# Moving steps of the second and third chunk in a fused attention and MLP kernel

## The chip, the cores and the metric

The kernel runs on one core of a Trainium2 chip. A core has a tensor engine (PE in the profile; PEld is its loading of weights), a vector engine (DVE), a scalar engine (ACT), a general engine that also issues transfers (POOL) and a sync engine that issues transfers (SP). Each takes its instructions in the order in which the program lists them and waits at an instruction until what it needs is there. Matrix products write to PSUM, eight banks that are numbered 0 to 7 here; the other data lie in SBUF. The metric is the device time of one execution in microseconds (us).

## What is computed

A linear attention with decay over 4 batches, 8 heads, 768 positions and head size 64, and behind it an MLP with a "snake" activation over the 3072 tokens. The reference, cut to its core:

```python
for b in range(nb):                     # 12 blocks of 64 positions
    sl = slice(b * block, (b + 1) * block)
    qb, kb, vb = (q[:, :, sl].copy(), k[:, :, sl].copy(), v[:, :, sl].copy())
    intra = np.einsum('bhic,bhjc->bhij', qb, kb) * Dmask[None]
    intra = np.einsum('bhij,bhjd->bhid', intra, vb)
    inter = np.einsum('bhid,bhde->bhie', qb * lam_pow[None], kv_state)
    out[:, :, sl] = intra + inter
    kb_dec = kb * rev_pow[None]
    kv_state = lam_block[None, :, None, None] * kv_state + np.einsum('bhsd,bhse->bhde', kb_dec, vb)
...
h = x @ w_in                            # 512 -> 2048
s = np.sin(alpha * h)
g = h + s * s / (alpha + 1e-09)
return (g @ w_out).astype(np.float32)   # 2048 -> 512
```

## The kernel before

**Tiling.** The 768 positions are cut into six chunks t = 0 to 5 of 128. A chunk of all four batches gives a group g = t of 512 tokens for the MLP. While PE does the MLP of group g, the attention of chunk g + 1 is spread between its products, so that its output `xt[g + 1]` is there when group g + 1 begins. A chunk has two halves of 64 positions (`blk`), and its batches come in two pairs (`pr`).

**The MLP.** For each of 16 slices f of the inner size, `hidden(g, f)` issues four products of 128x512 into one bank (L453), then on ACT the sine (L456) and, where `squarer` names ACT, the square (L461). `finish(g, f)` issues the square on DVE where `squarer` names DVE (L469), and always DVE's `gall` (L470), which reads the bank and so frees it. The second product is cut into units: `project(g, m, part)` is four products (L481) over `gall` f = 4 part to 4 part + 3 for the tokens of batch m. Units wait in the list `behind`; `run(n)` issues the next n. The unit with part 3 copies the sum out of PSUM (L488 on DVE or L490 on ACT) and queues the store. In group 0, `squarer` gives DVE the squares of f = 3, 5, 7, 9 and 11. The units of group 0 come in an order written out at L596; the last nine are (3,1), (0,2), (1,2), (2,2), (3,2), (3,3), (2,3), (0,3), (1,3).

**The attention of a chunk t.** 
- q and k are turned to have the head size in the partitions: on PE with a copy behind (`turn`, L275, copies L277 and L279; `turns_pair`, L289, copies L292), or by a transfer on SP's queue (`turn_by_dma`, L252).
- `decay_k` (POOL, L236) makes `kdec`; `states` (L369) multiplies it with v into four banks.
- `update(t, blk, pr)` adds this to the decayed state on DVE (L345; for chunk 1's second half four smaller instructions, L349), then POOL decays the new state for the next use (`decay_state`, L334) and casts it (`cast_state`, L338).
- `scores` (L389) multiplies k with q into F banks; `masks` (DVE, L396) reads them.
- `outputs_first` (L403) multiplies the states with q into O banks, all but one product; `outputs` adds that product and the masked scores with v (L428); `leave` (DVE, L435) writes `xt`.

Scores, states, turns and outputs of a chunk share banks. For chunk 1 the banks are passed by hand: its second pair's states use banks 4 and 2, its scores 5 and 0, its O banks 4 and 2 again. For later chunks they are `AB`, banks 4 to 7: states, the turned q, scores and O take them one after the other, and each must have been read before the next is written.

**The order around the change.** Group 0's loop over f (L598 to L626) also holds chunk 1's first pair of batches. Behind it stands a straight stretch for chunk 1's second pair (L627 to L659), where the calls `run(n)` place projection units of group 0 between the steps. Then the loop over g begins. In it, for group 1, `feed(g)` gives steps that are issued ahead of `hidden(g, i)`, `slots(g)` those behind it, then `run` issues as many units as i occurs in `units`, then `finish`. `own` names where units of group 1 itself are added to the list. `hidden(1, 11)` has chunk 2's `outputs_first` in its middle, behind its products and its sine.

**Loads.** `load` and `load_w_out` issue transfers on POOL's queue, which also does the decays and casts in program order. `load(t, nm, 2, 4)` of k and q are two transfers each (L101, L102).

Of the kernel before, what the change touches and what calls it, by code (L numbers as in the profile page):

```python
# [15 lines left out]
def kernel(  # L16
# [16 lines left out]
    NT = S // T  # L33
# [3 lines left out]
    NFC = DFF // P  # L37
# [53 lines left out]
    def load_w_out(i):  # L91
        nc.gpsimd.dma_start(out=w_out_sb[i][:],
                            in_=moe_w_out[i * 512:(i + 1) * 512, :].rearrange("(f p) d -> p f d", p=P))

    def load(t, nm, b0, b1):
        dst, src = NAT[nm]
        to = dst[t][:, b0:b1, :, :].rearrange("p b h e -> p (b h) e")
        by_head = src[b0:b1, :, t * T:(t + 1) * T, :].rearrange("b h p e -> p (b h) e")
        n = H * (b1 - b0)
        if t and nm != "v" and b0 == 2:  # L100
            nc.gpsimd.dma_start(out=to[:, 0:n - 1, :], in_=by_head[:, 1:n, :])  # L101
            nc.gpsimd.dma_start(out=to[:, n - 1:n, :], in_=by_head[:, 0:1, :])  # L102
        else:
            nc.gpsimd.dma_start(out=to, in_=by_head)  # L104
# [99 lines left out]
    V, G, A = nc.vector, nc.gpsimd, nc.scalar  # L204
# [17 lines left out]
    def home(t, blk):  # L222
        return SB[2 if blk else t % 2]
# [106 lines left out]
    def pair(tile, pr):  # L330
        return tile[:, 2 * pr:2 * pr + 2]

    def decay_state(n, pr):
        nc.gpsimd.tensor_tensor(out=pair(SD, pr), in0=pair(S_of[n], pr), op=ALU.mult,  # L334
                                in1=L64[:, pr].unsqueeze(1).unsqueeze(3).broadcast_to([P, 2, HP, D]))

    def cast_state(n, pr, dst):
        nc.gpsimd.tensor_copy(out=pair(dst, pr), in_=pair(S_of[n], pr))  # L338
# [94 lines left out]
    def leave(t, pr, blks=(0, 1)):  # L433
        for blk in blks:
            nc.vector.tensor_tensor(out=xview(t)[:, 2 * pr:2 * pr + 2, blk, :, :], in0=att["O", t, pr, blk],  # L435
                                    in1=Eb, op=ALU.mult)
# [4 lines left out]

    def squarer(g, f):
        if g == 0:
            return V if f in (3, 5, 7, 9, 11) else A
        return A

    H0 = (0, 1, 2, 3, 5, 6, 7, 4, 0, 1, 3, 5, 0, 1, 5, 0)
# [1 line left out]
    def hidden(g, f, between=None):  # L449
        hps = bank("hps", H0[f] if g == 0 else (0, 5, 4, 2)[f] if g == 1 and f < 4 else AB[0] if g == 1 and f == 15 else AB[f + 1] if g == 2 and f < 2 else HB[(f + 2) % 3] if g == 1 else HB[(16 * g + f + 1) % 3])  # L450
        w = w_in_sb[f // 4]
        for c in range(NDC):
            nc.tensor.matmul(out=hps[:], lhsT=w[:, c, (f % 4) * P:(f % 4 + 1) * P],  # L453
                             rhs=xt[g][:, c, :], start=(c == 0), stop=(c == NDC - 1))
        s_sb = mlps.tile([P, GRP], BF16, name="s_sb")
        nc.scalar.activation(out=s_sb[:], in_=hps[:], func=ACTF.Sin, scale=alpha_sb[:, f:f + 1])  # L456
        if between:
            between()
        s2 = mlps.tile([P, GRP], BF16, name="s2")
        if squarer(g, f) is A:  # L460
            nc.scalar.activation(out=s2[:], in_=s_sb[:], func=ACTF.Square)  # L461
        elif squarer(g, f) is G:
            nc.gpsimd.tensor_tensor(out=s2[:], in0=s_sb[:], in1=s_sb[:], op=ALU.mult)
        hps_of[g, f] = (hps, s_sb, s2)
# [19 lines left out]

    def store(g, m):
        o_sb = outp.tile([P, DM], FP32, name="o_sb")
        if g < NT - 2 and (g or m < 2):
            nc.vector.tensor_copy(out=o_sb[:], in_=ops_of.pop((g, m))[:])  # L488
        else:
            nc.scalar.copy(out=o_sb[:], in_=ops_of.pop((g, m))[:])  # L490
        held.append((m * S + g * T, o_sb))
        if g:
            put_held()

    def put_held():
        while held:
            row, o_sb = held.pop(0)
            nc.sync.dma_start(out=out[row:row + T, :], in_=o_sb[:])
# [93 lines left out]
    def run(n):  # L592
        for _ in range(min(n, len(behind))):
            behind.pop(0)()
# [3 lines left out]
    for f in range(NFC):  # L598
        hidden(0, f)
        if f in (1, 10):  # L600
            states1(0, f // 10, 2 if f == 10 else 4)
        if f == 10:
            decay_k(1, 0, 2)
            decay_state(1, 0)
            cast_state(1, 0, home(1, 0))
            load_w_out(2)
            load(1, "q", 2, 4)
            load_w_out(3)
            load(2, "v", 0, 2)
        if f in (11, 12):  # L610
            run(1)
        if f == 12:
            turns_pair(1, "k", 0, 4, (A, A))
        if f == 13:
            turn(1, "q", 0, 2, A)
            turn(1, "q", 1, 3, V)
        if f == 14:
            scores(1, (0,), (4, 2))
            masks(1, 0)
        if f == 15:  # L620
            run(1)
            states(1, (0,), (3, 4))
            finish(0, 14)
            update(1, 0, 0)
        if f != 14:
            finish(0, f)  # L626
# [11 lines left out]
    leave(1, 0)  # L638
    states(1, (1,), (4, 2))
    update(1, 0, 1)  # L640
    run(3)
    turn(1, "q", 2, 5, A)
    turn(1, "q", 3, 0, V)
    load(2, "k", 0, 2)
# [2 lines left out]
    scores(1, (1,), (5, 0))  # L647
    masks(1, 1)
    load(2, "k", 2, 4)
    run(1)  # L650
    outputs_first(1, (1,), (4, 2))
    load(2, "q", 0, 2)
    load(2, "q", 2, 4)
    run(1)
    outputs(1, (1,))
    leave(1, 1)
    run(1)
    decay_state(1, 0)
    pair_ready(2, 0)  # L659


    def slots(g):
        t = g + 1
        d = {i: [] for i in range(NFC)}
        if g == 1:
            at = dict(KV=6, F=9, O=12)
        else:
            at = dict(KV=4, F=8, O=12)
        d[at["KV"]] += [(states, t)]
        for n in range(4):  # L670
            d[at["KV"] + ((0, 0, 1, 2)[n] if g == 1 else n)] += [(update, t, n // 2, n % 2)]
        d[at["F"]] += [(scores, t), (masks, t, 0)]
        d[at["F"] + 1] += [(masks, t, 1)]
        d[at["O"]] += [(outputs, t), (leave, t, 0)]
        d[at["O"] + (g > 1)] += [(leave, t, 1)]
        return d

    def feed(g):
        t = g + 1
        d = {i: [] for i in range(NFC)}  # L680
        if g == 1:
            d[2] += [(turn_by_dma, 2, 0, "k"), (pair_ready, 2, 1), (decay_state, 1, 1), (turn_by_dma, 2, 1, "k"), (turn_by_dma, 2, 0, "q")]
            d[7] += [(put_held,)]
            d[8] += [(turns_pair, 2, "q", 2, AB[0], (A, A))]
        if t + 1 < NT:
            if g == 1:
                d[7] += [(new_chunk, 3)] + [(load, 3, nm, b, b + 2) for nm, b in (("v", 0), ("k", 0), ("v", 2))]
                d[8] += [(load, 3, nm, b, b + 2) for nm, b in (("k", 2), ("q", 0), ("q", 2))]
            else:
                a = 6 if g == 2 else 2  # L690
                d[a] += [(new_chunk, t + 1)] + [(load, t + 1, nm, b, b + 2) for nm, b in (("v", 0), ("k", 0), ("v", 2))]
                d[a + 2] += [(load, t + 1, nm, b, b + 2) for nm, b in (("k", 2), ("q", 0), ("q", 2))]
            d[12] += [(turn_by_dma, t + 1, 0, "k"), (turn_by_dma, t + 1, 1, "k")]
            d[13] += [(pair_ready, t + 1, 0)]
            d[14] += [(turn_by_dma, t + 1, 0, "q"), (turn_by_dma, t + 1, 1, "q")]
            d[15] += [(pair_ready, t + 1, 1)]
        return d

    for g in range(1, NT + 1):
        if g < NT:  # L700
            gall[g] = gbp.tile([P, NFC, GRP], BF16, name="gall")
        at = slots(g) if g + 1 < NT else {}
        fd = feed(g) if g + 1 < NT else {}
        if g + 1 < NT:
            new_xt(g + 1)
        own = {5: (0, 0), 8: (0, 1), 13: (0, 2)} if g == 1 else {}
        units = [1, 3, 5, 8, 13] if g == 1 else [i for i in range(NFC) if g > 2 or i not in (0, 1, 3)]
        for i in range(NFC):
            if g == NT and not behind:
                break  # L710
            if i in own:
                queue_units(g, [own[i]])
            for a in fd.get(i, []):
                a[0](*a[1:])
            if g > 1 and g + 1 < NT and i == 12:
                outputs_first(g + 1)
            if g < NT:
                hidden(g, i, (lambda: outputs_first(2)) if (g, i) == (1, 11) else None)
            for a in at.get(i, []):
                a[0](*a[1:])  # L720
            run(units.count(i))
            if g < NT:
                finish(g, i)
        if g < NT:
            queue_units(g, [(m, part) for m in range(B - 1 if g == NT - 1 else B) for part in range(4)][len(own):])
# [31 lines left out]
```

## Time and profile before

| what | value |
|---|---|
| times of three runs | 211.74, 211.49, 210.94 us; median 211.49 |
| the profiled execution's own time | 210.82 us |
| its span, first to last instruction | 209.0 us |
| granted PE clock | 0.997 of full speed |
| chain that ended last, share by engine | PE 80%, DVE 11%, ACT 4%, DMA 2% |
| gall on DVE (L470) | 96 instructions, 745 ns each |
| sine (L456) and square (L461) on ACT | 684 and 629 ns each |

The profile is of one execution. Its views used here: the page (busy time by engine), the instructions in order of time with like neighbours merged, busy time by stretch, and the chain of waits that ended last. Starts are in us from the span's start. The modelled end of a product lies behind the start of the next one, as products are pipelined, so the prediction works with starts.

### The profile page before, as it was taken

The numbers are of one execution on the slowest core, as the hardware profiler recorded it, in microseconds if no ns is written. First come the engines' busy times: TensorE is split into PE (matmuls) and PEld (weight loads), VectorE is DVE, ScalarE is ACT, GpSimd is POOL, SyncE is SP. The second block draws the span as 40 slices with busy tenths as digits, with TensorE's granted clock in tenths as the row PEclk, the third lists the DMA queues.
The fourth block names the chain that finished last, engine by engine and source line by source line (L and its number), as shares of the span: only waits on it lengthen the run. The fifth ranks groups of instructions, "written<-read, shape, count | busy, mean of one in ns | idle before, by whom it ended". The sixth has DMA issues, their size and how long they took to land.

```text
span 209.0 us, 5363 instructions
## 1 busy us (share of the span) xinstructions
PE 201.0 (96%) x2243; PEld 98.7 (47%) x2243; DVE 132.9 (64%) x218; ACT 143.1 (68%) x239; POOL 107.0 (51%) x111
## 2 busy tenths in 40 slices
PE   7999998999998999999999999999999999999993
PEld 2664444544453544445444444445444444444452
DVE  6794999473778868968547968556868544444000
ACT  4788989213999699765776775776675787887121
POOL 8989939979939993999986850002000000000000
PEclk9999999999999999999999999999999999999998
DMA  7999999999997999699999998701101101110212
GB/s 140 156 170 207 207 159 178 185 179 135 127 311 50 145 127 161 99 175 161 106 150 145 209 103 130 174 0 53 50 3 53 50 0 50 55 50 0 100 59 93
DMA packets 98794, 24.60 MB, mean 118 GB/s; under 512 B 90946, under 2 KB 95826, under 8 KB 98770
## 3 DMA queue, kind: packets, MB, share of 16 engines
q0 software_dynamic: 76176, 13.24, 86.7%
q1 hardware_dynamic: 20512, 10.50, 24.4%
q10 hardware_dynamic: 2082, 0.52, 1.4%
q8 instruction: 17, 0.28, 0.5%
q14 instruction: 7, 0.06, 0.1%
HBM read 27.27 MB, written 6.29 MB: 161 GB/s over the span
## 4 chain that ended last, share of the span: by engine, by line
PE 80%; DVE 11%; ACT 4%; DMA 2%; issue 1%; ACTq 0%
PE ops L481 37%; PE hps L453 33%; DVE gall L470 4%; DMA raw_k<-in_k_dram 2%; PE O_ps L403 2%; ACT s_sb L456 2%; ACT s L461 2%; PE hps L505 2%; DVE s L469 2%; DVE STm L304 2%; PE KV_ps L369 2%; PE O_ps L428 1%; PE F_ps L389 1%; DVE STm L396 1%; DVE xt L316 1%
## 5 line engine op out<-in xcount | busy, mean ns | idle before, releaser
L470 DVE SCALAR_TENSOR_TENSOR gall<-s,r_sb,hps 128x512 bf16<-128x512 bf16 x96 | 71.2, 745 | 45.0 <-ACT s L461 44.8
L453 PE MATMUL hps<-xt,w_in 128*128 128x512 bf16 x384 | 95.7, 379 | 1.2 <-DVE gall L470 0.5
L481 PE MATMUL ops<-w_out,gall 128*128 128x512 bf16 x368 | 92.4, 380 | 0.4 <-DVE gall L470 0.4
L456 ACT ACTIVATE s_sb<-hps,alpha_sb 128x512 bf16<-128x512 f32 x96 | 65.2, 684 | 32.1 <-PE hps L453 31.9
L461 ACT ACTIVATE s<-s_sb 128x512 bf16<-128x512 bf16 x91 | 57.3, 629 | 2.9
L453 PEld LDWEIGHTS <-w_in 128*128 128x128 bf16 x384 | 36.6, 98 | 44.1 <-issue 1.9
L481 PEld LDWEIGHTS <-gall 128*128 128x128 bf16 x368 | 34.6, 98 | 41.2 <-DVE gall L470 0.9
L236 POOL TENSOR_TENSOR kdec<-kn,R 128x1024 bf16<-128x1024 bf16 x12 | 22.8, 1924 | 3.2 <-DMA kn<-in_k_dram 3.2
L338 POOL CAST sb<-S 128x512 bf16<-128x512 f32 x20 | 12.3, 618 | 21.8 <-DVE S L345 20.6
L334 POOL TENSOR_TENSOR SD<-S,L 128x512 f32<-128x512 f32 x16 | 17.1, 1066 | 10.6 <-DVE S L345 10.5
L435 DVE TENSOR_TENSOR xt<-O_ps,Etab 128x512 bf16<-128x512 f32 x20 | 12.8, 685 | 6.3 <-PE O_ps L428 6.3
L104 POOL DMA_DIRECT2D vn<-in_v_dram x13 | 14.8, 1153 | 0.5 <-DMA w_in<-in_moe_w_in_dram 0.5
L396 DVE TENSOR_TENSOR STm<-F_ps,C 128x512 bf16<-128x512 f32 x20 | 12.8, 685 | 0.1
L488 DVE COPY o_sb<-ops 128x512 f32<-128x512 f32 x14 | 9.6, 689 | 4.2 <-PE ops L481 4.2
L490 ACT COPY o_sb<-ops 128x512 f32<-128x512 f32 x9 | 5.2, 577 | 9.7 <-PE ops L481 9.7
L345 DVE TENSOR_TENSOR S<-SD,KV_ps 128x512 f32<-128x512 f32 x16 | 10.8, 683 | 0.4 <-PE KV_ps L369 0.3
L128 PE MATMUL hps<-fill 128*128 128x256 bf16 (+1 forms) x40 | 9.7, 352 | 1.5 <-DVE fill L121 1.5
L277 ACT COPY QKT<-T_ps 128x512 bf16<-128x512 bf16 x9 | 5.2, 584 | 6.4 <-PE T_ps L275 6.4
L104 POOL DMA_DIRECT2D qn<-in_q_dram x8 | 8.8, 1099 | 0.3 <-issue 0.3
L104 POOL DMA_DIRECT2D kn<-in_k_dram x7 | 7.7, 1093 | 0.1
L403 PEld LDWEIGHTS <-sb 64*64 64x64 bf16 x320 | 4.3, 108 | 6.3 <-issue 6.3
L403 PE MATMUL O_ps<-QKT,sb 64*64 64x64 bf16 x320 | 5.9, 195 | 1.0 <-DVE STm L396 1.0
(75 smaller groups left out, 114.5 us busy)
## 6 DMA issues: line engine op xcount, KB each, us to landing
out_dram<-o_sb SPq DMA_DIRECT2D x23, 256.0 KB, 2.2
vn<-in_v_dram POOLq DMA_DIRECT2D x11, 256.0 KB, 7.5
w_out<-in_moe_w_out_dram POOLq DMA_DIRECT2D x4, 512.0 KB, 11.3
w_in<-in_moe_w_in_dram POOLq DMA_DIRECT2D x3, 512.0 KB, 11.6
kn<-in_k_dram POOLq DMA_DIRECT2D x5, 256.0 KB, 7.0
qn<-in_q_dram POOLq DMA_DIRECT2D x5, 256.0 KB, 9.9
kn<-in_k_dram POOLq DMA_DIRECT2D x5, 240.0 KB, 6.4
qn<-in_q_dram POOLq DMA_DIRECT2D x5, 240.0 KB, 9.0
```

What stands on the lines that cost most here:

```text
L104: nc.gpsimd.dma_start(out=to, in_=by_head)
L236: nc.gpsimd.tensor_tensor(out=kdec[t][:, b0:b1, :, :], in0=kn[t][:, b0:b1, :, :], in1=R[:, o:o + H].unsqueeze(1).unsqueeze(3).broadcast_to ...
L334: nc.gpsimd.tensor_tensor(out=pair(SD, pr), in0=pair(S_of[n], pr), op=ALU.mult, in1=L64[:, pr].unsqueeze(1).unsqueeze(3).broadcast_to([P, ...
L338: nc.gpsimd.tensor_copy(out=pair(dst, pr), in_=pair(S_of[n], pr))
L396: nc.vector.tensor_tensor(out=st[:, hd], in0=att["F", t, pr, hd], op=ALU.mult, in1=of_mask(C64, t, pr, hd).unsqueeze(1).broadcast_to([P, 2 ...
L403: nc.tensor.matmul(out=att["O", t, pr, blk][halves(h % 2), u, h // 2, :], lhsT=home(t, blk)[halves(half), 2 * pr + m // HP, m % HP, :], rh ...
L435: nc.vector.tensor_tensor(out=xview(t)[:, 2 * pr:2 * pr + 2, blk, :, :], in0=att["O", t, pr, blk], in1=Eb, op=ALU.mult)
L453: nc.tensor.matmul(out=hps[:], lhsT=w[:, c, (f % 4) * P:(f % 4 + 1) * P], rhs=xt[g][:, c, :], start=(c == 0), stop=(c == NDC - 1))
L456: nc.scalar.activation(out=s_sb[:], in_=hps[:], func=ACTF.Sin, scale=alpha_sb[:, f:f + 1])
L461: nc.scalar.activation(out=s2[:], in_=s_sb[:], func=ACTF.Square)
L470: nc.vector.scalar_tensor_tensor(out=gall[g][:, f, :], in0=s2[:], scalar=r_sb[:, f:f + 1], in1=hps[:], op0=ALU.mult, op1=ALU.add)
L481: nc.tensor.matmul(out=ops[:], lhsT=gall[g][:, f, m * P:(m + 1) * P], rhs=w_out_sb[part][:, f % 4, :], start=(f == 0), stop=(f == NFC - 1))
```

## The change

The diff moves work between engines and along the queues; no operation is added or left out.

```diff
     def squarer(g, f):
         if g == 0:
-            return V if f in (3, 5, 7, 9, 11) else A
+            return V if f in (1, 3, 5, 7, 9) else A
         return A
...
-        if g < NT - 2 and (g or m < 2):
+        if g < NT - 2 and (g or m < 3):
             nc.vector.tensor_copy(out=o_sb[:], in_=ops_of.pop((g, m))[:])
...
             cast_state(1, 0, home(1, 0))
+            load(1, "q", 2, 4)
             load_w_out(2)
-            load(1, "q", 2, 4)
             load_w_out(3)
...
     update(1, 0, 1)
-    run(3)
+    run(1)
     turn(1, "q", 2, 5, A)
     turn(1, "q", 3, 0, V)
     load(2, "k", 0, 2)
     run(1)
     update(1, 1, 1)
     scores(1, (1,), (5, 0))
     masks(1, 1)
     load(2, "k", 2, 4)
-    run(1)
     outputs_first(1, (1,), (4, 2))
     load(2, "q", 0, 2)
     load(2, "q", 2, 4)
-    run(1)
+    run(2)
     outputs(1, (1,))
     leave(1, 1)
-    run(1)
-    decay_state(1, 0)
+    run(2)
     pair_ready(2, 0)
...
         if g == 1:
-            at = dict(KV=6, F=9, O=12)
+            at = dict(KV=5, F=9, O=12)
...
-        d[at["F"]] += [(scores, t), (masks, t, 0)]
-        d[at["F"] + 1] += [(masks, t, 1)]
+        if g > 1:
+            d[at["F"]] += [(scores, t), (masks, t, 0)]
+        d[at["F"] + (g > 1)] += [(masks, t, 1)]
...
-            d[2] += [(turn_by_dma, 2, 0, "k"), (pair_ready, 2, 1), (decay_state, 1, 1), (turn_by_dma, 2, 1, "k"), (turn_by_dma, 2, 0, "q")]
+            d[2] += [(turn_by_dma, 2, 0, "k"), (pair_ready, 2, 1), (decay_state, 1, 0), (decay_state, 1, 1), (turn_by_dma, 2, 1, "k"), (turn_by_dma, 2, 0, "q")]
             d[7] += [(put_held,)]
             d[8] += [(turns_pair, 2, "q", 2, AB[0], (A, A))]
+            d[9] += [(scores, 2), (masks, 2, 0)]
         if t + 1 < NT:
             if g == 1:
-                d[7] += [(new_chunk, 3)] + [(load, 3, nm, b, b + 2) for nm, b in (("v", 0), ("k", 0), ("v", 2))]
-                d[8] += [(load, 3, nm, b, b + 2) for nm, b in (("k", 2), ("q", 0), ("q", 2))]
+                d[6] += [(new_chunk, 3)] + [(load, 3, nm, b, b + 2) for nm, b in (("v", 0), ("k", 0), ("v", 2))]
+                d[7] += [(load, 3, nm, b, b + 2) for nm, b in (("k", 2), ("q", 0), ("q", 2))]
...
-        own = {5: (0, 0), 8: (0, 1), 13: (0, 2)} if g == 1 else {}
-        units = [1, 3, 5, 8, 13] if g == 1 else [i for i in range(NFC) if g > 2 or i not in (0, 1, 3)]
+        own = {8: (0, 0), 10: (0, 1), 13: (0, 2)} if g == 1 else {}
+        units = [1, 3, 4, 8, 10, 13] if g == 1 else [i for i in range(NFC) if g > 2 or i not in (0, 1, 3)]
```

Put in the order of PE's work: in the straight stretch one unit instead of three stands ahead of q's turn, scores and `outputs_first` follow each other directly, and two units stand behind each of `outputs_first` and `outputs`; six units of group 0 run there instead of seven. In group 1 the three left run behind f = 1, 3 and 4, the group's own first units behind f = 8, 10 and 13 instead of 5, 8 and 13. Chunk 2's states come behind f = 5 instead of f = 6, its scores ahead of f = 9 instead of behind it. On DVE both pairs of masks of chunk 2 then lie between the `gall` of f = 8 and that of f = 9, and the copy of unit (2,3) comes to it from ACT. On POOL the load of q's second pair goes ahead of that of the third slice of w_out, a decay of the state goes behind the two `kdec` of chunk 2, and chunk 3's loads go one step of the loop ahead. SP's order is the same.

## The prediction

> **What bounds the kernel now.** I read the engine table of the page first, then a table of busy time by stretch, then the instructions in order of time where the tensor engine (PE) pauses (start and length in us, engine, line, and in brackets the idle time before and what ended it). A group of four PE products of 128x512, 0.865 us, is called a block below: (2.76 - 0.38)/11 = 0.216 us each, from the row of twelve at 41.81 further down and the 0.39 of a single one at 63.39.
>
> ```profile
> span 209.0 us, 5363 instructions
> PE 201.0 (96%) x2243; PEld 98.7 (47%) x2243; DVE 132.9 (64%) x218; ACT 143.1 (68%) x239; POOL 107.0 (51%) x111
> 69.10:80.00 10.90, 10.90 (x178) 5.28 (x170) 8.04 (x14) 9.61 (x17) 10.02 (x10) 1.00 2.43 139
> ```
>
> PE is busy 96% of the span, and from 69.1 us on it has no gap (10.90 of 10.90; columns are length, then PE, PEld, DVE, ACT, POOL). The amount of PE work doesn't change. So the change is worth the PE pauses it removes ahead of 69.1 less those it makes, and I walk PE through its new order. The profiled run took 210.82 us, 1.82 more than its span and 0.67 less than the median of 211.49; I make the sum against the span and carry the difference over.
>
> **The squares of group 0.** f = 1 moves from ACT to DVE, f = 11 from DVE to ACT.
>
> ```profile
> 29.64 0.69 ACT L456 ACTIVATE s_sb<-hps,alpha_sb 128x512 bf16<-128x512 f32 x1 [0.60 <-PE hps L453]
> 29.72 2.13 DVE L469 TENSOR_TENSOR s<-s_sb 128x512 bf16<-128x512 bf16 x1
> 32.69 1.02 PE L453 MATMUL hps<-xt,w_in 128*128 128x512 bf16 x4 [0.47 <-DVE gall L470]
> 33.18 0.57 ACT L277 COPY QKT<-T_ps 128x512 bf16<-128x512 bf16 x1
> 33.79 0.39 PE L389 MATMUL F_ps<-QKT 64*64 64x64 bf16 x25
> ```
> ```profile
> 29.60:33.80 4.20, 3.65 (x30) 2.02 (x29) 4.16 (x6) 4.09 (x8) 4.13 (x4) 1.00 1.84 187
> ```
>
> The square of f = 11 took 2.13 us on DVE, and f = 14's products then waited 0.47 for a bank (0.63 in starts, since a modelled end lies 0.16 behind the next start). That wait goes. But the next 64x64 work, the scores at 33.79, starts 0.04 after ACT's copy of q (33.18 + 0.57 = 33.75), and ACT was busy 4.09 of the 4.20 us before it. That copy doesn't come sooner: its row of ACT work starts at 29.64 with f = 12's sine, which waits for PE. PE comes to the scores 0.63 sooner and waits there 0.63 longer. I cost this part at nothing. The added square fits into the 0.60 of ACT idle ahead of 29.64, and ACT is relieved of f = 1's before. On DVE, the square of f = 1 lies ahead of an in-order row that PE doesn't wait for.
>
> **Second chunk: 41.8 to 50.6.** One unit (a block) of the projection moves out of this stretch into the loop behind it; scores and O-first become adjacent, and two units follow each.
>
> ```profile
> 41.81 2.76 PE L481 MATMUL ops<-w_out,gall 128*128 128x512 bf16 x12
> 42.84 0.68 DVE L345 TENSOR_TENSOR S<-SD,KV_ps 128x512 f32<-128x512 f32 x1
> 44.41 0.61 PE L275 MATMUL T_ps<-iden,qn 128*128 128x128 bf16 x8
> 44.85 1.03 PE L481 MATMUL ops<-w_out,gall 128*128 128x512 bf16 x4
> 45.06 0.42 DVE L279 COPY QKT<-T_ps 128x512 bf16<-128x512 bf16 x1 [1.54 <-PE T_ps L275]
> 45.40 1.11 DVE L349 SCALAR_TENSOR_TENSOR S<-S,L,KV_ps 128x128 f32<-128x128 f32 x4
> 45.81 0.45 PE L389 MATMUL F_ps<-QKT 64*64 64x64 bf16 x32
> 46.19 1.04 PE L481 MATMUL ops<-w_out,gall 128*128 128x512 bf16 x4
> 48.75 0.46 PE L428 MATMUL O_ps<-STm,vn 64*64 64x64 bf16 x32
> 49.14 1.04 PE L481 MATMUL ops<-w_out,gall 128*128 128x512 bf16 x4
> ...
> 50.61 1.89 PE L453 MATMUL hps<-xt,w_in 128*128 128x512 bf16 x8 [0.43 <-DVE xt L435]
> ```
> ```profile
> 47.23 0.62 PE O_ps L403 x31
> ```
>
> New walk: block (3,1) 41.81 to 42.68; the turn of q, 0.44 (44.41 to 44.85), to 43.12; block (0,2) to 43.98; a change to 64x64 costs 0.10 (45.81 less 44.85 + 0.865), so scores at 44.08, and their 32 products take some 0.27 of the 0.38 to 46.19, the rest being the way back to 128 rows. O-first would start at 44.35. Its second product writes the bank that L349 reads. DVE is in order: L345 until 43.52, the copy L279 until some 43.86, L349 (overlapping 0.08) until 44.90. So PE goes on at 44.95, a **new wait of 0.60** that before was covered by a block: L349 ended at 46.51, O-first came after 47. O-first from there 0.61 (the chain's 0.62 for the visit): 45.56; two units to 47.29, with 0.10 to 47.39; outputs, 0.39 (48.75 to 49.14), to 47.78; two units to 49.51. xt came 1.86 after the outputs' start (50.61 less 48.75), so at 49.25: covered by 0.26, and the wait at 50.61 (0.61 in starts, 49.14 + 0.865 = 50.00) is gone. Before, with one unit more: 50.61 - 0.865 = 49.74. **Gain 0.23**: 0.61 and one change of shape (about 0.2) less 0.60.
>
> **The two loads that change places.** q must be there at 42.68, w_out(2) at 43.12.
>
> ```profile
> L92 POOL DMA_DIRECT2D w_out<-in_moe_w_out_dram x1: 823/823/823, 33.3 to 33.3; - x1
> DMA to landing us min/median/max: 8.0/8.0/8.0
> ```
> ```profile
> L101 POOL DMA_DIRECT2D qn<-in_q_dram x1: 1204/1204/1204, 34.1 to 34.1; - x1
> DMA to landing us min/median/max: 9.0/9.0/9.0
> ```
> ```profile
> DMA to landing us min/median/max: 8.0/9.6/13.0
> ```
>
> w_out(2) landed at 41.3, q at 43.1. Swapped, q is issued at 33.3 and w_out(2) behind q's two issues at about 35.1 (estimate: 1.2 and half of it). If the queue keeps its order and its rate, the second of the two lands where the second did, 43.1: just in time, and a delay up to 0.60 goes into the wait for L349. I take zero. The ends: w_out(2) after 8.0 us again, nothing; after the 13.0 of the slowest of the three loads behind 20 us, 48.05, a wait of 4.9. This is the largest unknown. The row says that landings kept the order of issue; the Trainium skill, "DMA: Bandwidth & Descriptors", section "Two DMAs through the same engine are not ordered", says that nothing orders transfers across the 16 DMA engines. By that rule w_out(2) could share its time with w_out(3) behind it, which is the rival on the slower side below; by the row the sum stays.
>
> **Second group: 50.6 to 69.1.**
>
> ```profile
> 59.34 0.73 PE L369 MATMUL KV_ps<-vn,kdec 64*64 64x64 bf16 x64
> 60.01 1.04 PE L453 MATMUL hps<-xt,w_in 128*128 128x512 bf16 x4
> 61.08 0.69 ACT L456 ACTIVATE s_sb<-hps,alpha_sb 128x512 bf16<-128x512 f32 x1 [0.29 <-PE hps L453]
> 62.34 1.05 ACT L292 COPY QKT<-T_ps 128x512 bf16<-128x512 bf16 x2
> 63.39 0.39 PE L481 MATMUL ops<-w_out,gall 128*128 128x512 bf16 x1 [0.39 <-DVE gall L470]
> 64.67 0.75 DVE L470 SCALAR_TENSOR_TENSOR gall<-s,r_sb,hps 128x512 bf16<-128x512 bf16 x1 [0.46 <-ACT s L461]
> 65.33 1.28 DVE L396 TENSOR_TENSOR STm<-F_ps,C 128x512 bf16<-128x512 f32 x2
> 67.07 0.21 PE L403 MATMUL O_ps<-QKT,sb 64*64 64x64 bf16 x1
> 68.53 0.66 PE L403 MATMUL O_ps<-QKT,sb 64*64 64x64 bf16 x59 [0.38 <-DVE STm L396]
> 69.12 1.04 PE L453 MATMUL hps<-xt,w_in 128*128 128x512 bf16 x4
> ```
>
> Two waits go: 0.55 at 63.39 (0.39 and 0.16), where unit (0,1) ran before f = 7's gall; and 1.43 between 67.07 and 68.53, where O-first waited for the masks to free its banks. New walk from f0 at 49.51: six f and three units, 9 x 0.865, to 57.29; states at 57.39, 0.67 (59.34 to 60.01), so f6 at 58.06, f7 58.93, turn 59.79, f8 60.23, unit (0,0) 61.10 to 61.96, scores possible at 62.06. They write the bank that the two copies L292 read. ACT: f6's sine 1.07 after f6's start (61.08 less 60.01), 59.13; f7's sine 1.26 later (61.08 to 62.34 is a sine and a square), 60.39; the copies end 2.31 behind that sine, as before (63.39 less 61.08): 62.70. Scores at 62.75, a **new wait of 0.69**. Then f9 63.42, f10 64.28, unit (0,1) 65.15, f11 66.01, O-first possible at 66.98. DVE: f8's gall 1.28 behind the copies (64.67 less 63.39), 63.98; four masks from 64.64, 1.28 a pair, to 67.13. O-first's last bank is free at 67.18, **0.20 of wait** left; its last group takes 0.59 (68.53 to 69.12), to 67.77; f12 needs f9's gall, which DVE now has behind the masks, 67.05 + 0.75 = 67.80: f12 at 67.85. Against 69.12 that is **1.27 sooner**. By terms: 0.23 + 0.55 + 1.43 - 0.69 - 0.20 - 0.08 = 1.24; I take 1.25. The copy of unit (2,3) from PSUM moves from ACT to DVE, under the wait of DVE for ACT's squares.
>
> **What hides the rest.** The state decay that POOL has moved, and chunk 3's loads one step sooner:
>
> ```profile
> 52.82 3.79 POOL L236 TENSOR_TENSOR kdec<-kn,R 128x1024 bf16<-128x1024 bf16 x2
> 60.90 1.04 POOL L334 TENSOR_TENSOR SD<-S,L 128x512 f32<-128x512 f32 x1 [3.29 <-DVE S L345]
> 75.34 3.79 POOL L236 TENSOR_TENSOR kdec<-kn,R 128x1024 bf16<-128x1024 bf16 x2
> 79.53 0.66 PE L369 MATMUL KV_ps<-vn,kdec 64*64 64x64 bf16 x58
> ```
>
> Even if POOL were no sooner, kdec ends a decay sooner than at 56.61, at 55.6, and the two decays at 57.7, ahead of DVE's first need of them at about 57.9. Uncovered they would cost up to 1.04. Behind that POOL waited 3.29 for DVE at 60.90; this need now comes some 2 us sooner, so the six loads, and kdec at 75.34, follow sooner. They must: kdec of chunk 3 ended at 79.13 and PE took it at 79.53; PE will be there at 78.28. Everything after is in step with PE.
>
> **Rivals.** (1) The squares pay too: f = 14 waited for DVE, and PE has 0.63 more. Against it stands the copy at 33.75. Gain 1.88, 209.6 us. (2) POOL or chunk 3's k stays where it was: states of chunk 3 wait for kdec until 79.2, 0.9 us, and gain 0.35 is left, 211.1 us. For it: a margin of only 0.4 before. Against: the 3.29 of idle that POOL loses. (3) Slower: w_out(2) lands late and holds unit (0,2). It eats the gain from a landing at 43.12 + 0.60 + 1.25 = 44.97 on; at 48.05 it costs 4.35 net of the cover, so 3.1 us slower, 214.6. (4) The change doesn't do what it says: each wait only moves from one place to the next, ACT and DVE running as a chain from f6 to f12 (8.7 of my 9.8 us there are theirs), so 211.5.
>
> **How the numbers follow.** Forecast: span 209.0 - 1.25 = 207.75, the profiled run 209.57, at the median 210.2 us; its own range 209.8 to 210.8, from plus or minus 0.5 for the three new waits. Chances: forecast 0.50, rival (1) 0.08, (2) 0.20, (3) 0.12, (4) 0.10. What a measurement can tell from no change is about 0.5%, 1.06 us, so faster means below 210.43: most of the forecast (0.42), all of (1) and little of (2): 0.52. Slower means above 212.55: (3), 0.12. The rest, 0.36, is the same. Range 209.4 to 212.0: it holds (1), (2) and (4), and leaves out the late end of (3) and the tails of the others, some 0.17 in all.
>
> **What will show it.** Right: the scores at 33.8 still start just behind ACT's copy; O-first of the second chunk splits after its first product at about 44.4, with DVE's L349 as releaser; no wait for xt ahead of f0 at 49.5; scores of the third chunk released by ACT's L292 near 62.7; f12 near 67.9. Wrong: PE waiting for w_out at 43, for kdec near 78, or scores at 33.8 well sooner.

## The result and the profile after

The changed kernel took 209.83 us (median of six runs, 209.50 to 210.26), the kernel before 211.30 (six runs beside them, 210.83 to 211.74): a ratio of 0.9932 with a 95% interval of 0.9913 to 0.9951, 1.4 us faster. A second set of seven runs, below, gave 0.9920 (0.9890 to 0.9951). The ratios leave out executions that took over 1.5% longer than the fastest of the same kernel, the medians do not; only the last two versions of the table below have such executions, six of twelve and four of nine. The prediction had 210.2 us, a gain of 1.25, and a range of 209.4 to 212.0.

The engine table of the profiled execution (209.97 us in all) looks like that of before. PE is still the engine that is busy almost without a break. (Its 2213 product records stand against 2243 weight loads: 30 products have no record in this trace, which is why some rows below count one product less.)

```profile
span 208.2 us, 5336 instructions
PE 199.1 (96%) x2213; PEld 99.6 (48%) x2243; DVE 131.9 (63%) x219; ACT 142.5 (68%) x238; POOL 106.7 (51%) x111
```

The span is only 0.8 shorter than the 209.0 of before, in part since this execution came later to the first projection unit. That unit starts between 27.69 and 28.46 us in the fourteen traces of this case, which are of one execution each; the two of the changed kernel differ by 0.16. A measure that is free of this runs between two places that every version has: from U, the first projection unit of group 0, to X, the first unit behind the twenty products at 72 us. Both are L481 rows of PE in the instructions in order of time. First the two of before:

```profile
27.70 1.04 PE L481 MATMUL ops<-w_out,gall 128*128 128x512 bf16 x4
...
76.84 1.03 PE L481 MATMUL ops<-w_out,gall 128*128 128x512 bf16 x4
```

Then the same two of after:

```profile
27.95 1.03 PE L481 MATMUL ops<-w_out,gall 128*128 128x512 bf16 x4
...
75.73 1.03 PE L481 MATMUL ops<-w_out,gall 128*128 128x512 bf16 x4
```

From U to X before: 76.84 - 27.70 = 49.14 us; after: 75.73 - 27.95 = 47.78, so 1.36 less. With U 0.25 later, and a new pause of 0.32 at 117 us that is told of below, that is 1.36 - 0.25 - 0.32 = 0.79 of the span.

The stretch of the first squares, PE in order of time (start, length, line, idle time before it and what ended it):

```profile
31.85 0.61 PE L275 MATMUL T_ps<-iden,qn 128*128 128x128 bf16 x8
32.30 1.03 PE L453 MATMUL hps<-xt,w_in 128*128 128x512 bf16 x4
34.03 0.35 PE L389 MATMUL F_ps<-QKT 64*64 64x64 bf16 x21 [0.71 <-ACT QKT L277]
```

f = 14 (32.30) now follows the turn of q at once, and what PE won it lost again in front of the scores, which ACT's copy of q releases. (The row of the scores ends where the view was cut.) They start 34.03 - 27.95 = 6.08 behind U; before it was 33.79 - 27.70 = 6.09.

The second chunk's second pair, PE and then DVE:

```profile
42.92 0.68 PE L275 MATMUL T_ps<-iden,qn 128*128 128x128 bf16 x8
43.52 1.02 PE L481 MATMUL ops<-w_out,gall 128*128 128x512 bf16 x4
44.47 0.45 PE L389 MATMUL F_ps<-QKT 64*64 64x64 bf16 x32
44.75 0.19 PE L403 MATMUL O_ps<-QKT,sb 64*64 64x64 bf16 x1
45.17 0.66 PE L403 MATMUL O_ps<-QKT,sb 64*64 64x64 bf16 x30 [0.23 <-DVE S L349]
...
49.73 1.24 PE L453 MATMUL hps<-xt,w_in 128*128 128x512 bf16 x4
```
```profile
43.67 0.42 DVE L279 COPY QKT<-T_ps 128x512 bf16<-128x512 bf16 x1
44.01 1.11 DVE L349 SCALAR_TENSOR_TENSOR S<-S,L,KV_ps 128x128 f32<-128x128 f32 x4
```

O-first splits behind its first product, until DVE's L349 is done (44.01 + 1.11 = 45.12): 45.17 - 44.75 = 0.42 of waiting. The wait for xt ahead of group 1's first products (49.73) is gone.

The second group, PE in order of time:

```profile
61.31 1.03 PE L481 MATMUL ops<-w_out,gall 128*128 128x512 bf16 x4
62.93 0.73 PE L389 MATMUL F_ps<-QKT 64*64 64x64 bf16 x64 [0.60 <-ACT QKT L292]
...
67.16 0.87 PE L403 MATMUL O_ps<-QKT,sb 64*64 64x64 bf16 x63
68.02 1.02 PE L453 MATMUL hps<-xt,w_in 128*128 128x512 bf16 x3
...
78.41 0.74 PE L369 MATMUL KV_ps<-vn,kdec 64*64 64x64 bf16 x64
```

The scores could have started at 61.31 + 0.865 + 0.10 = 62.27 and started at 62.93, behind ACT's copies: 0.66 of waiting. O-first runs through in 0.86, where before it took 69.12 - 67.07 = 2.05 with its waits. Chunk 3's states at 78.41 wait for nothing.

Chunk 4's scores, far behind the change, are the one thing that is new and was not foreseen:

```profile
116.90 0.45 PE L389 MATMUL F_ps<-QKT 64*64 64x64 bf16 x32
117.51 0.45 PE L389 MATMUL F_ps<-QKT 64*64 64x64 bf16 x32 [0.17 <-PE F_ps L389]
```

They came in one piece before. Now their second half starts 0.61 behind the first instead of 0.29 (44.75 - 44.47 for the same 32 products), just behind the landing of the second transposed q at 117.38. The view of that transfer's line (L252: count, issue time in ns, starts) says how long it took:

```profile
L252 SPq DMA_TRANSPOSE QKT<-qn x1: 2382/2382/2382, 107.5 to 107.5; - x1
...
DMA to landing us min/median/max: 9.9/9.9/9.9
```

### The profile page after: what moved, and what is told of

Same layout as the page of the kernel before. It is cut to its first block, busy times and chain, and to the rows that moved or that the text cites. A ratio compares the mean times of both kernels' runs of the same rounds, so it can differ in the third digit from the quotient of the medians.

```text
span 208.2 us, 5336 instructions
## 1 busy us (share of the span) xinstructions
PE 199.1 (96%) x2213; PEld 99.6 (48%) x2243; DVE 131.9 (63%) x219; ACT 142.5 (68%) x238; POOL 106.7 (51%) x111
## 4 chain that ended last, share of the span: by engine, by line
PE 85%; DVE 4%; ACT 3%; DMA 3%; issue 2%; ACTq 0%
PE hps L453 38%; PE ops L481 37%; DMA raw_k<-in_k_dram 3%; PE O_ps L403 2%; PE hps L505 2%; PE F_ps L389 2%; DVE STm L304 2%; PE KV_ps L369 1%; PE O_ps L428 1%; ACT s_sb L456 1%; DVE xt L316 1%; ACT s L461 1%; ACT QKT L292 1%; PE T_ps L275 1%; DVE S L349 1%
## 5 line engine op out<-in xcount | busy, mean ns | idle before, releaser
L453 PE MATMUL hps<-xt,w_in 128*128 128x512 bf16 x369 | 94.2, 379 | 1.4 <-DVE xt L316 0.3
L481 PE MATMUL ops<-w_out,gall 128*128 128x512 bf16 x353 | 90.3, 379 | 0.9 <-issue 0.3
L481 PEld LDWEIGHTS <-gall 128*128 128x128 bf16 x368 | 34.8, 98 | 40.5 <-issue 0.6
L488 DVE COPY o_sb<-ops 128x512 f32<-128x512 f32 x15 | 10.3, 689 | 4.2 <-PE ops L481 4.1
L490 ACT COPY o_sb<-ops 128x512 f32<-128x512 f32 x8 | 4.6, 576 | 12.0 <-PE ops L481 12.0
L104 POOL DMA_DIRECT2D qn<-in_q_dram x8 | 8.8, 1099 | 0.3 <-issue 0.3
L101 POOL DMA_DIRECT2D qn<-in_q_dram x5 | 6.1, 1218 | 1.4 <-DMA qn<-in_q_dram 1.4
```

The lines of the kernel that those rows point to most:

```text
L481: nc.tensor.matmul(out=ops[:], lhsT=gall[g][:, f, m * P:(m + 1) * P], rhs=w_out_sb[part][:, f % 4, :], start=(f == 0), stop=(f == NFC - 1))
```

## The experiments

All versions compute the whole of the reference. Ratios are against the kernel before, run on the same chip beside them (medians 211.02 to 211.30); "U to X" is the measure above, from each version's profiled execution.

| version | median, us | ratio (95%) | U to X, us | against before |
|---|---|---|---|---|
| before | 211.30 | 1 | 49.14 | |
| changed | 209.83 | 0.9932 (0.9913 to 0.9951) | 47.78 | -1.36 |
| changed, again | 209.59 | 0.9920 (0.9890 to 0.9951) | 47.78 | -1.36 |
| squares alone | 210.98 | 0.9997 (0.9981 to 1.0012) | 49.13 | -0.01 |
| straight stretch alone | 210.76 | 0.9989 (0.9970 to 1.0009) | 48.89 | -0.25 |
| second group alone | 209.85 | 0.9938 (0.9917 to 0.9958) | 48.04 | -1.10 |
| changed, w_out(2) ahead of q again | 209.93 | 0.9934 (0.9915 to 0.9954) | 48.29 | -0.85 |
| changed, chunk 2's scores behind f = 9 again | 210.16 | 0.9965 (0.9951 to 0.9979) | 48.46 | -0.68 |
| changed, chunk 5's loads later | 209.70 | 0.9934 (0.9901 to 0.9967) | 47.79 | -1.35 |
| changed, last copy of q on ACT | 209.58 | 0.9929 (0.9906 to 0.9952) | 47.67 | -1.47 |
| changed, masks sooner | 209.64 | 0.9912 (0.9878 to 0.9946) | 47.29 | -1.85 |
| changed, first copy of q on DVE | 209.09 | 0.9908 (0.9894 to 0.9923) | 47.17 | -1.97 |
| masks sooner, chunk 4's loads sooner | 212.37 | 0.9982 (0.9942 to 1.0021) | 47.37 | -1.77 |
| the same, both copies of q moved | 210.94 | 0.9937 (0.9904 to 0.9970) | 46.82 | -2.32 |

**The three parts, each alone in the kernel before.** Their gains add up to the whole: 0.01 + 0.25 + 1.10 = 1.36. In the times only the third part is clear of noise.

The squares:

```diff
-            return V if f in (3, 5, 7, 9, 11) else A
+            return V if f in (1, 3, 5, 7, 9) else A
```

> The kernel before with the squares of f = 1 and f = 11 exchanged, nothing else. My theory: f = 14's products no longer wait for a bank, but the scores that follow still start just behind ACT's copy of q, so PE waits there about 0.78 us instead of 0.15 and the time is unchanged (ratio 1.000, within 0.1 us). Rival (the squares pay by themselves): the scores start 0.6 us sooner and the ratio is 0.997.

The time and U to X did not move. The scores' row of PE in this version, in order of time:

```profile
33.90 0.44 PE L389 MATMUL F_ps<-QKT 64*64 64x64 bf16 x32 [0.71 <-ACT QKT L277]
```

f = 14 went out at 32.16 right behind the turn; its wait now stands in front of the scores, at ACT's copy. The rival that the squares pay falls.

The straight stretch:

```diff
-        if g < NT - 2 and (g or m < 2):
+        if g < NT - 2 and (g or m < 3):
...
+            load(1, "q", 2, 4)
             load_w_out(2)
-            load(1, "q", 2, 4)
...
-    run(3)
+    run(1)
...
-    run(1)
     outputs_first(1, (1,), (4, 2))
...
-    run(1)
+    run(2)
     outputs(1, (1,))
     leave(1, 1)
-    run(1)
+    run(2)
...
-        units = [1, 3, 5, 8, 13] if g == 1 else ...
+        units = [1, 3, 4, 5, 8, 13] if g == 1 else ...
```

> The kernel before with the straight stretch of the change alone (the loads of q and w_out exchanged, one unit ahead of q's turn, scores and O-first adjacent, two units behind each; three units of group 0 left for group 1, behind f = 1, 3 and 4; group 1's own steps as before). My theory: f = 0 of group 1 starts 0.2 us sooner than a unit's length explains, O-first waits some 0.4 to 0.6 us for L349, and the pauses of group 1 at unit (0,1) and at O-first stay nearly whole; ratio 0.998 to 0.999. Rival (the stretch carries the gain): ratio 0.995 or less.

U to X fell by 0.25, which the times alone can't tell from nothing. O-first waited from 44.51 to 45.02 for L349, and the two waits of the second group stayed. The rival that this stretch carries the gain falls: a ratio of 0.995 lies outside the interval.

The second group (states, scores, masks, units and chunk 3's loads a step sooner, the moved state decay):

> The kernel before with the changes of the second group alone (states behind f = 5, scores ahead of f = 9, group 1's own units behind f = 8, 10 and 13, chunk 3's loads a step sooner, the decay behind kdec); the straight stretch, the squares and the two loads as before. My theory: the pauses at unit (0,1), 0.55, and at O-first, 1.43, go and about 0.7 to 1.0 comes back ahead of scores and O-first: about 1.0 us faster, ratio 0.995. Rival (the pauses only move): ratio 0.998 or more.

This part carries 1.10 of the 1.36 us. The wait for xt at 50 stayed, and the long pauses of O-first went. What came back stands in other places than in the changed kernel: 0.24 ahead of the scores, and 0.44 ahead of f = 8, for a `gall` (61.21 - 60.33 - 0.44, from the start of the turn), together 0.68 against the 0.66 ahead of the scores there.

**The two loads.** The changed kernel with `load_w_out(2)` ahead of `load(1, "q", 2, 4)`, as before.

> The changed kernel with the third slice of w_out loaded ahead of q again. My theory: q lands near 43.2 instead of 40.8, the turn of q and with it DVE's copy and L349 start 0.3 to 0.6 us later, so 0.3 to 0.6 us of the gain is lost (ratio to before 0.995 to 0.9965). Rival (the exchange is worth nothing, since PE waits for L349 anyway): same time as the changed kernel.

The turn's row of PE in order of time:

```profile
43.28 0.62 PE L275 MATMUL T_ps<-iden,qn 128*128 128x128 bf16 x8 [0.43 <-DMA qn<-in_q_dram]
```

Here the turn of q waits for its load, and U to X loses 0.51 of the gain. So in this trace the exchange is needed for the rest. The times don't show it: the ratio is 0.9934, where the theory had 0.995 to 0.9965, and they do not exclude the rival's "same time".

**The scores put back.** The changed kernel with chunk 2's scores behind f = 9.

```diff
-        if g > 1:
-            d[at["F"]] += [(scores, t), (masks, t, 0)]
-        d[at["F"] + (g > 1)] += [(masks, t, 1)]
+        d[at["F"]] += [(scores, t), (masks, t, 0)]
+        d[at["F"] + 1] += [(masks, t, 1)]
...
-            d[9] += [(scores, 2), (masks, 2, 0)]
```

> Chunk 2's scores and first masks go back behind f = 9; the rest is the changed kernel. By the prediction's terms this gives up the O-first wait of 1.43 and gets back the new scores wait of 0.69: 0.74 us slower than the changed kernel, f12 of group 1 some 0.7 later, ratio to before 0.9955. Rival: DVE's row of masks and galls sets the end of the masks in both orders, so the two waits only trade places: no wait ahead of the scores (near 63.0), some 1 us of wait inside O-first, released by L396, f12 within 0.25 of the changed kernel's, ratio 0.992 to 0.9935.

U to X grew by 0.68, near the 0.74 of the prediction's two terms, and the ratio is 0.9965. PE in order of time:

```profile
62.76 1.03 PE L453 MATMUL hps<-xt,w_in 128*128 128x512 bf16 x4
63.71 0.74 PE L389 MATMUL F_ps<-QKT 64*64 64x64 bf16 x64
...
67.08 0.21 PE L403 MATMUL O_ps<-QKT,sb 64*64 64x64 bf16 x1
68.01 0.22 PE L403 MATMUL O_ps<-QKT,sb 64*64 64x64 bf16 x3 [0.72 <-DVE STm L396]
68.61 0.66 PE L403 MATMUL O_ps<-QKT,sb 64*64 64x64 bf16 x59 [0.38 <-DVE STm L396]
```

The scores wait for nothing (62.76 + 0.865 + 0.10 = 63.72), and from O-first's first product to its last long row it is 68.61 - 67.08 = 1.53, nearly all of it waiting for DVE's masks. The rival, that the two waits only trade places, falls: one is more than twice the other.

**The changed kernel again, and three single edits in it.** First without an edit, to see how much one execution says.

> The changed kernel once more, to have it beside the next three on one chip. My theory: the pauses ahead of 72 us as in its first profile (0.78 ahead of the scores at 34, 0.42 inside O-first at 45, 0.67 ahead of the scores at 63), and again a pause inside the scores of chunk 4 near 117.5, because the transposed q of its second pair of batches lands there whatever PE's pace is. Rival (that pause was a chance of one execution): no pause at 117.5.

U to X came out the same to 0.01. Chunk 4's scores ran in one piece here: the theory falls on this point and the rival stands, the pause at 117 comes in some executions and not in others.

> The changed kernel with chunk 5's loads four steps later in group 3 (behind f = 6 and 8 instead of f = 2 and 4), as in group 2. My theory: the transfers that share the queues with chunk 4's transposes go, these land 1 us or more ahead of 117.4, the pause inside chunk 4's scores goes, and the time is 0.2 to 0.4 us below the changed kernel's. Rival (chunk 5's loads, now late, hold chunk 5's kdec or transposes): pauses near 140 or 148 and no gain.

```diff
-                a = 6 if g == 2 else 2
+                a = 6 if g in (2, 3) else 2
```

Chunk 5's six loads then go out from 113.7 us on instead of 99.6, and chunk 4's transposes of q have only stores beside them. The view of their line in this version:

```profile
L252 SPq DMA_TRANSPOSE QKT<-qn x2: 1232/1232/1232, 103.0 to 106.7; - x2
...
DMA to landing us min/median/max: 3.0/3.8/4.5
```

They took 4.5 and 3.0 us to land instead of 9.3 and 9.9 in the changed kernel. So it is the loads of chunk 5 beside it that hold the second q of chunk 4 back. Chunk 5's own states and scores have no pause in this trace. The time is that of the changed kernel, so the 0.2 to 0.4 us of the theory did not show: over the runs the pause costs too little to be measured.

> The changed kernel with the copy of the last turned q of chunk 1 on ACT instead of DVE. My theory: L349 starts a copy sooner (about 0.34 us), so the pause inside O-first near 45 shrinks from 0.42 to about 0.1, and f = 0 of group 1 starts 0.3 us sooner. Rival (ACT's second copy, behind its first, comes too late for the scores): the pause moves ahead of or into the scores and nothing is gained.

```diff
-    turn(1, "q", 3, 0, V)
+    turn(1, "q", 3, 0, A)
```

With the copy off DVE, L349 comes sooner, and O-first takes 45.54 - 44.68 = 0.86 where without a wait it took 0.61. That is worth 0.11 from U to X instead of 0.3, and nothing that the times can show.

> The changed kernel with chunk 2's last q turned into bank 6 instead of 4, and with the first pair's masks on DVE ahead of the gall of f = 8. My theory: the first pair's scores need not wait for ACT's two copies, the second pair's still do: the pause of 0.67 ahead of the scores near 63 becomes about 0.35; DVE does two masks in the 1.27 us in which it waits for ACT, so O-first and f = 12 do not wait; in all 0.4 to 0.7 us sooner at f = 14. Rival (ACT's chain of sines, squares and copies sets f = 12 anyway): nothing gained.

```diff
-            d[8] += [(turns_pair, 2, "q", 2, AB[0], (A, A))]
-            d[9] += [(scores, 2), (masks, 2, 0)]
+            d[8] += [(turns_pair, 2, "q", 2, AB[2], (A, A))]
...
             run(units.count(i))
+            if (g, i) == (1, 8):
+                scores(2)
+                masks(2, 0)
             if g < NT:
                 finish(g, i)
```

With q turned in another bank, only the second half of the scores waits for ACT's copies, and DVE does the first pair of masks ahead of the gall of f = 8. PE in order of time, with chunk 4's scores as the last two rows:

```profile
62.01 0.45 PE L389 MATMUL F_ps<-QKT 64*64 64x64 bf16 x32
62.68 0.44 PE L389 MATMUL F_ps<-QKT 64*64 64x64 bf16 x32 [0.22 <-ACT QKT L292]
...
66.61 0.71 PE L403 MATMUL O_ps<-QKT,sb 64*64 64x64 bf16 x63
...
116.26 0.45 PE L389 MATMUL F_ps<-QKT 64*64 64x64 bf16 x32
117.47 0.45 PE L389 MATMUL F_ps<-QKT 64*64 64x64 bf16 x32 [0.76 <-DMA QKT<-qn]
```

O-first has no wait left and U to X is 0.49 better than the changed kernel, as the theory had it; but in this execution 117.47 - 116.26 - 0.29 = 0.92 was lost behind X to chunk 4's q, with the DMA now named as the releaser.

**A first copy of q that doesn't gate.** The changed kernel, with the copy in front of chunk 1's scores on DVE.

```diff
-            turn(1, "q", 0, 2, A)
+            turn(1, "q", 0, 2, V)
```

> Changed kernel, with the copy of q that gates chunk 1's scores near 34 moved from ACT to the idle DVE. Theory: the scores start 0.6 to 0.75 sooner after the products of f = 14, so the exchange of squares now brings its time at that place, but PE then stands 0.5 to 0.7 us ahead of w_out(2), which in the changed kernel landed 0.04 before its unit began: the DMA engines are full from 24 us on, so the landing stays at 43.3 to 43.5 and the time is lost in front of unit (0,2). Group 1's f0 stays 33.0 to 33.1 us behind group 0's first product, ratio to before 0.991 to 0.993. Rival: the landing moves along with the sooner PE, and nothing takes the 0.65 back: f0 at 32.4 to 32.5, ratio 0.989.

This version has the lowest median of all, 209.09 us, below the changed kernel too, though the intervals of the two ratios overlap; U to X is 0.61 better. PE in order of time:

```profile
32.28 1.03 PE L453 MATMUL hps<-xt,w_in 128*128 128x512 bf16 x4
33.23 0.44 PE L389 MATMUL F_ps<-QKT 64*64 64x64 bf16 x32
...
42.12 0.68 PE L275 MATMUL T_ps<-iden,qn 128*128 128x128 bf16 x8
43.18 1.02 PE L481 MATMUL ops<-w_out,gall 128*128 128x512 bf16 x4 [0.38 <-DMA w_out<-in_moe_w_out_dram]
...
44.41 0.67 PE L403 MATMUL O_ps<-QKT,sb 64*64 64x64 bf16 x31
```

The scores follow f = 14 at once, 0.78 sooner behind it than in the changed kernel (0.95 against 1.73). PE then does stand in front of w_out(2), for some 0.5 us up to 43.18, as the theory said. But the conclusion from it was wrong: the wait for L349 behind it (0.42 in the changed kernel) is gone, because DVE went on meanwhile. One wait stands in the place of the other, so most of what was won stays: from f = 14 to group 1's first products it is 48.97 - 32.28 = 16.69 us against 49.73 - 32.30 = 17.43. By the theory's own sign, the start of f = 0 behind group 0's first product, the result lies between the two sides: 32.69 us, where the changed kernel has 33.09.

**Chunk 4's loads sooner.** The version with the masks sooner, and:

```diff
-                a = 6 if g == 2 else 2
+                a = 4 if g == 2 else 2
```

> The version with scores and masks of chunk 2 behind the unit of f = 8 and their q in another bank, which lost 0.65 of its gain at 117 us waiting for a transfer of chunk 4's q; here chunk 4's six loads are issued two steps sooner (steps 4 and 6 of group 2), where POOL sat idle for 4 us. Theory: the pause at 117 came from the late issue of the loads: the second pair of q lands 1.5 us or more sooner than 117.3, the pause goes, the earlier gain stays, span 207.4, ratio to before 0.989 to 0.990. Rival: the DMA engines' rate sets the landing, whenever the loads are issued: the pause of 0.5 us or more stays or comes back at chunk 5, ratio 0.992.

Both sides missed: the time is no better than that of before. The twelve times ran from 208.93 to 217.32 us; the profiled execution, 213.7, is one of the longer ones and shows a pause at chunk 3:

```profile
85.55 0.45 PE L389 MATMUL F_ps<-QKT 64*64 64x64 bf16 x32
88.75 0.45 PE L389 MATMUL F_ps<-QKT 64*64 64x64 bf16 x32 [2.76 <-DMA QKT<-qn]
89.13 1.56 PE L481 MATMUL ops<-w_out,gall 128*128 128x512 bf16 x3
90.48 1.91 PE L453 MATMUL hps<-xt,w_in 128*128 128x512 bf16 x4
92.19 1.39 PE L481 MATMUL ops<-w_out,gall 128*128 128x512 bf16 x4
93.42 1.03 PE L453 MATMUL hps<-xt,w_in 128*128 128x512 bf16 x4
```

The pause is 88.75 - 85.55 - 0.29 = 2.91 us, and it cost more than that. The three blocks behind it took 93.42 - 89.13 = 4.29 us instead of 3 x 0.865 = 2.60: the granted clock was 0.51 from 89.5 to 93.0, and 1.00 before and behind. Pause and lower clock together are 4.6 us. From X to the end this execution has 136.7 us, where the nine traces without a pause behind X have 132.1 to 132.2.

What this does not show: no shorter execution of this version was profiled, so whether they lack the pause, and why four of the six shortest are no faster than before, stays open. And chunk 4's second q landed at 118.38, later than the 117.33 of the version with the masks sooner; it held nobody up because PE came 4.6 us later. So it is not shown that sooner loads take the pause at 117 away.

The transposes of chunk 3's q were issued at 77.2 and 78.6, as in the changed kernel (77.2 and 79.0), but now among the first three loads (77.0 to 79.3). The views of L252 in this version, and then in the changed kernel:

```profile
L252 SPq DMA_TRANSPOSE QKT<-qn x2: 1232/1627/2022, 77.2 to 78.6; - x2
...
DMA to landing us min/median/max: 7.5/8.8/10.1
```
```profile
L252 SPq DMA_TRANSPOSE QKT<-qn x2: 1231/1232/1232, 77.2 to 79.0; - x2
...
DMA to landing us min/median/max: 4.1/4.5/4.9
```

In this execution it is the same harm at a sooner place. POOL sits idle from 77.2 to 81.5 us in the changed kernel, but that is idle time of the queue, not of the 16 DMA engines. Their busy share there in tenths, in 40 slices of 0.35 us from 76 to 90 us:

```profile
DMA  9999997999969980099920000000004999999999
```

They are busy almost throughout until 81 us; their long idle stretch is from 83.4 to 86.5.

> The version with chunk 4's loads two steps sooner, and also both copies of q moved (that of batch 0 to DVE, that of batch 3 to ACT). Theory, with w_out(2) as the limit near 43.4: only some 0.1 us beyond the version without the copies, span 207.3, ratio 0.9885 to 0.990. Rival, if the copy of batch 0 pays in full: 0.75 us beyond it, ratio 0.986.

U to X is the shortest of all, 2.32 less than before and 0.55 less than in the version without the copies, between the 0.1 of the theory and the 0.75 of the rival. In the profiled execution, 212.78 and again one of the longer ones, the same pause at 85 (2.4, and behind it three blocks in 4.28) takes it back; the shortest times, 208.47 and 208.77, are the lowest seen. The version that would put together what helped (masks sooner, both copies moved, and chunk 5's loads later in place of chunk 4's sooner) was not run.

## Why the prediction came out right

**The squares, costed at nothing.** Right, alone (-0.01) and for its reason: the copy of q gates the scores. The first copy on DVE shows the other side of it: with the gate moved, the 0.6 is there to be had. What the prediction took as fixed, though, the 2.13 us of the square of f = 11, belongs to some executions only (last section); in the version with the second group alone, where that square took 0.42, the scores start 34.11 - 28.02 = 6.09 behind U all the same.

**The straight stretch, 0.23.** Measured alone 0.25. Of its terms, the new wait for L349 was 0.51 there and 0.42 and 0.46 in the two traces of the changed kernel, and not 0.60, and in the changed kernel it was 43.52 - 42.92 = 0.60 from the turn of q to the unit behind it and not the 0.44 taken from before; PE came 0.16 later to the same DVE chain and so waited that much less. The two errors cancel, since DVE's end sets the time.

**The two loads, costed at zero, with a late w_out(2) as the slower rival.** Right, and for the reason given. q landed at 40.69 and 40.85, but w_out(2) at 43.48, 0.04 ahead of its unit at 43.52. The turn's products started some 0.055 apart, the last at 43.38, so PE could have gone on near 43.44 and waited some 0.08 for w_out(2). That went into the wait for L349, as the prediction said of a delay up to 0.60. In the two versions with the first copy of q on DVE, PE comes sooner and waits there, 0.5 and 0.8 us.

**The second group, 0.55 + 1.43 - 0.69 - 0.20 - 0.08 = 1.01.** Measured alone 1.10, with its new waits in other places (above). In the changed kernel the wait for the copies was 0.66 (0.69 foreseen), and O-first took 0.86, 0.22 more than the 67.25 - 66.61 = 0.64 that it takes without a wait in the version with the masks sooner (0.20 foreseen); the trade of O-first's wait for that of the scores, 1.43 - 0.69 = 0.74, measured 0.68 when undone.

**The covers.** Chunk 3's `kdec` was in time (states at 78.41 without a wait): the rival of 211.1 falls. The rival that waits only move falls with the table: 1.36 us stay.

**What was wrong: "Everything after is in step with PE."** PE's own row is: from X to the end the nine traces without a pause behind X have 132.11 to 132.23 us, the kernel before among them. The transfers are not, and the sum gave them no term. Chunk 4's second q had 118.04 + 0.29 - 116.19 = 2.1 us in hand before; in the two traces of the changed kernel it held PE up by 0.32 in one and was in time in the other, and it held PE up by 0.92 with the masks sooner. But PE's gain alone doesn't decide this: with the first copy on DVE, where PE had gained more still, that q landed at 113.8, 2.8 us ahead of its use, and with the scores put back, where PE had gained less, it held PE up by 0.8. The landing differs by 5 us (113.8 to 119.1) among the eleven traces in which the loads of chunks 4 and 5 have the same places in the program. That chunk 5's loads hold it back is shown; what makes it differ so stays open. The missing term cost 0.32 and nothing in the two traces, within the range given. The other terms were too small by 0.12 (1.36 against 1.24).

## What to carry to other kernels

Count a wait that goes only up to the next thing that gates the engine behind it, and walk the order on until a full stretch has no wait left. Where two things gate the same step, taking one away brings nothing until the other moves too, and a new wait ahead of an old one takes from the old one before it takes from the time. When the engine that bounds gets faster, look up the slack of every transfer behind it, and in more than one execution. Idle time of a queue was not idle time of the DMA engines here, so look at both before a load is moved. A long pause of PE can cost more than its length: look at the granted clock behind it.

## What the runs showed of the hardware

**Who starts first decides what a square costs.** The same DVE instruction, beside the same POOL instruction, in the kernel before and in the version with the second group alone (the squares are alike in both), DVE and POOL by their starts:

```profile
29.67 1.90 POOL L236 TENSOR_TENSOR kdec<-kn,R 128x1024 bf16<-128x1024 bf16 x1 [3.18 <-DMA kn<-in_k_dram]
29.72 2.13 DVE L469 TENSOR_TENSOR s<-s_sb 128x512 bf16<-128x512 bf16 x1
```
```profile
29.78 0.42 DVE L469 TENSOR_TENSOR s<-s_sb 128x512 bf16<-128x512 bf16 x1
30.00 1.96 POOL L236 TENSOR_TENSOR kdec<-kn,R 128x1024 bf16<-128x1024 bf16 x1 [3.18 <-DVE gall L470]
```

Behind POOL's start by 0.05 us the square took 2.13 us, ahead of it by 0.22 it took 0.42. A third trace with these squares, that of the straight stretch alone, has it 0.24 behind POOL's start, with 1.93; in both long cases it ended some 0.28 behind POOL's instruction. The bank wait of f = 14 that the prediction read from before's profile was absent from the execution with the 0.42. The Trainium skill, "SBUF — State Buffer", section "Who interferes with whom", says that issue order decides who blocks when both use the port pair that DVE and GpSimd (POOL here) share; these rows agree.

**A pause of PE was followed by a lower clock.** Behind the pauses of 2.9 and 2.4 us at chunk 3 the granted clock was 0.51 and 0.58 over 89.5 to 93.0, and three blocks took 4.29 and 4.28 us instead of 2.60. Behind the pause of 0.92 at 117 in the version with the masks sooner it stayed at 1.00 (116 to 120).

**Loads on POOL's queue and transposes on SP's queue slow each other.** Chunk 3's transposes took 4.1 and 4.9 us without chunk 4's loads beside them and 7.5 and 10.1 with the first three, and these loads took 8.0 to 10.9 us beside them and 5.9 to 7.3 in the changed kernel, where they go out behind them. Chunk 4's transposes took 9.3 and 9.9 with chunk 5's loads and 4.5 and 3.0 without. The Trainium skill, "DMA: Bandwidth & Descriptors", section "Issuing engines are not separate DMA queues", says that transfers of all engines run on the same 16 DMA engines and interleave; these landings agree.
